# Threshold attention and hash-routed experts: GpSimd's indirect transfers given in other steps of a head pair

## The chip, the cores and the metric

The kernel runs on one core of one Trainium2 chip. The metric is device time in microseconds of one execution, and of several executions the median is given. A core has engines that run side by side, each with its own instruction queue, and wait for each other through semaphores: TensorE (PE: matrix products and transposes, into the accumulator memory PSUM), VectorE (DVE), ScalarE (ACT), GpSimd (POOL) and SyncE (SP), which here only issues transfers. SBUF is the on-chip working memory; DRAM tensors lie outside. In this kernel GpSimd computes small things and issues the indirect transfers, whose row addresses come from a table.

## The reference

Two blocks follow each other. The first is attention with a threshold, for 8 batches, 8 heads, 576 positions and a head width of 64. Of each row of scores only those within `tau` of the row's maximum count:

```python
scores = scale * np.matmul(q, k.transpose(0, 1, 3, 2))
thresh = np.max(scores, axis=-1, keepdims=True) - tau
scores = np.where(scores >= thresh, scores, -1000000000.0)
scores = scores - np.max(scores, axis=-1, keepdims=True)
attn = np.exp(scores)
attn = attn / (np.sum(attn, axis=-1, keepdims=True) + 1e-09)
return np.matmul(attn, v).astype(np.float32)
```

The result is laid out as `x`, 4608 tokens by 512. In the second block each token goes to one of 8 experts, chosen by its id alone:

```python
expert_idx = token_ids * np.int64(2654435761) % np.int64(E)
...
    h = np.maximum(xe @ w1[e], 0.0)
    out[mask] = h @ w2[e]
```

Since the choice of expert depends only on the ids, the routing can be worked out while attention still runs.

## The kernel before, in words

**Pairs and steps.** Attention works on two heads at a time. There are 32 head pairs: `p` counts them, eight batches for each of four pairs of heads (`hp`). A pair is worked in `NS = 5` steps, and one loop (L710) runs over all steps: `n` is the step in all, `p, s = divmod(n, NS)`, `LAST` is 160. Step 0 takes the last 64 query rows of both heads, steps 1 to 4 take 128 query rows each, for each head in turn. The order of instructions on every engine is the order in which this loop gives them (`manual_schedule`), so that the position of a line in the loop body is the position in the queue.

**The work on a step's rows.** `score` (L221) multiplies q and k on TensorE, one step ahead. `negate` (L238) on VectorE takes the scores from PSUM, negated, into `ns`, with their minimum in `nmx`; when a step's last head is negated, GpSimd adds the threshold, `thr` (L253). `expo` (L256) is the exponential on ScalarE. `mask` (L263) on VectorE multiplies the exponentials by the comparison with `thr` and sums them up. It is called one step later: in step n it works on step n-1, after the negations of step n. Two steps later `turn_w` (L285) transposes the weights on TensorE and `put_wT` (L294) copies them from PSUM on ScalarE. `av_part` (L305) multiplies them with v, `put_oT` (L327) copies out, `turn_o` (L331) transposes the result back in step 0 two pairs later, and `put_xm` (L347), in that same step 0, scales it on VectorE and writes it to the DRAM tensor `x_scratch` with three transfers on SP (L358, L363).

**SP's queue.** In step 0 of a pair, SP is given the loads of k and q for the pair after next (`load_pair`), those of v for the next pair (`load_v`), and after them x's writes. In step 2 of pairs 20 and 24 it is given the 2 MB load of the first and second expert's `w1`, in step 2 of pairs 22 and 26 those of `w2`.

**GpSimd's queue in a pair.** In step 1 it has `add_eps` (L338, two small operations) and `scale_k` (L214, k of the next pair), both ahead of that step's threshold. Each of the five steps has one threshold. At the end of a step, behind the threshold, stand the indirect transfers:

- *Scatters* (`scatters`, L539). When the route is known (`placed`), 36 scatters write token numbers into two slot tables in DRAM, alternately, one for each call. Each waits for the scatter before last, which wrote the same table. Behind them the same generator gives, at later calls, SP's reading of the tables and two small VectorE operations; then `routed` is set. `if s != 1 and placed` (L800) calls it in steps 0, 2, 3 and 4. The first scatter is that of pair 13, step 2, the last that of pair 22, step 0.
- *Early gathers* (`fetch_early`, L677). For the first expert, the first three quarters of its rows of x (`hp` 0 to 2; 5 groups of 128 slots, so 15 gathers of 64 KB) are fetched while the last quarter is still computed. A gather names all of `x_scratch`, so it waits for every write to it given before, and a write given after it waits for the gather. They start when `n > G0` (130, the start of pair 26), and are given in steps 3 and 4 (L802) and at the very start of step 0 (L713), ahead of that step's loads and of x's writes.

The last quarter's five gathers (L821) come when attention is over. Then follow the experts, 0 to 7, with loads, gathers and scatters of their own.

Of the kernel before, what the change touches and what calls it, by code (L numbers as in the profile page):

```python
# [20 lines left out]
def kernel(  # L21
# [29 lines left out]
    NS = 5  # L51
# [72 lines left out]
    def fetch_0(kt, hp):  # L124
        gather(x_rows, xg_bufs[kt][:, P * hp:P * hp + P], gidx_0[:, kt, hp:hp + 1])
# [18 lines left out]
    with tc.tile_pool(name="a_q", bufs=1) as a_q, \  # L144
# [59 lines left out]
        def load_v(p):  # L204
            hp, b = divmod(p, B)
            v_sb = v_bufs[p % 3]
            rows = v[b].rearrange("s h d -> s (h d)")[:, hp * P:hp * P + P]
            nc.sync.dma_start(out=v_sb[:, 0:4],
                              in_=rows[0:TAIL].rearrange("(c p) m -> p c m", p=P))
            for j in range(2):  # L210
                half = slice(64 * j, 64 * j + 64)
                nc.sync.dma_start(out=v_sb[half, 4, half], in_=rows[TAIL:S, half])
# [5 lines left out]
        def heads(n):  # L218
            return 1 if n % NS == 0 else 2
# [317 lines left out]
        placed, routed = [], []  # L537
# [139 lines left out]
        def fetch_early(n):  # L677


            if n > G0 and early:  # L680
                assert routed
                fetch_0(*early.pop(0))

        def fill(n):
            for _ in range(n):
                next(h_pieces, None)

        with tc.manual_schedule():
            make_identity(nc, ident[:])

            tr = ps_tr.tile([P, 2, 512], FP32, name="tr")
            for _ in range(17):
                nc.tensor.transpose(tr[:, 0, 0:P], ident[:], ident[:])
            nc.gpsimd.dma_start(out=tau_in[:],
                                in_=bass.AP(tensor=tau.tensor, offset=0, ap=[[0, P], [1, 1]]))

            nc.vector.tensor_scalar(out=k_scale[:], in0=tau_in[:], scalar1=0.0, scalar2=SCALE,
                                    op0=ALU.is_ge, op1=ALU.mult)  # L700
            nc.vector.tensor_scalar(out=kts[0][:, 0], in0=kts[0][:, 0], scalar1=k_scale[:],
                                    scalar2=None, op0=ALU.mult)
            nc.scalar.activation(kts[0][:, 1], kts[0][:, 1], AF.Copy, scale=k_scale[:])
            nc.vector.tensor_scalar(out=drop[:], in0=tau_in[:], scalar1=0.0, scalar2=3e38,  # L704
                                    op0=ALU.is_lt, op1=ALU.mult)
            nc.vector.tensor_tensor(out=drop[:], in0=drop[:], in1=tau_in[:], op=ALU.max)
            constants()
            next(pieces)
            score(0, 0)
            for n in range(LAST + NS + 1):  # L710
                p, s = divmod(n, NS)
                m = n - 2
                if s == 0:  # L713
                    fetch_early(n)
                if s == 0 and p + 2 < NP:
                    load_pair(p + 2)
                if s == 0 and p + 1 < NP:
                    load_v(p + 1)
                if s == 2 and p in (20, 24):
                    load_w1(p // 4 - 5)  # L720
                if s == 2 and p in (22, 26):
                    load_w2((p - 22) // 4)

                if (s == 3 and p > 0 or s == 2 and p in (9, 11, 13)) and not placed:
                    next(pieces)
                if s == 1 and 3 <= p < 2 + KT:
                    nc.sync.dma_start(out=xg_bufs[p - 2][:], in_=xg_bufs[0][:])

                if s == 1 and 2 + KT <= p < 2 + KT + N // DIN:
                    r0 = DIN * (p - 2 - KT)  # L730
                    nc.sync.dma_start(
                        out=x_dram[r0:r0 + DIN, DIN - P:].rearrange("(t p) m -> p t m", p=P),
                        in_=xg_bufs[0][:].rearrange("p (t m) -> p t m", m=P))
                q = p - 1
                if s == 1 and 0 <= q < NP:
                    add_eps(q)
                if s == (1 if p else 3) and p + 1 < NP:
                    scale_k(p + 1)
                if s == 2 and 0 <= q < NP:
                    nc.vector.reciprocal(recs[q][:], recs[q][:])  # L740
                if n == LAST + NS:
                    fill(2)
                if s == 0 and p >= 2:
                    turn_o()
                if n == LAST:
                    for k in (0, 2):
                        tr = ps_sc.tile([P, 2, 512], FP32, name="sc")
                        early_xT(tr, k, k + 2, 0, CO - 1)
                if s in (1, 2) and 0 <= q < NP and n != LAST + 1:
                    av_part(q, 0, ((0, 1, 2), (3, 4))[s - 1])  # L750
                if n < LAST and s in (1, 2):
                    negate(n, 0)
                    expo(n, 0)
                if s == 2 and 0 <= q < NP:
                    put_oT(0)
                if n > LAST:
                    fill(1)
                turned = 0 <= m < LAST
                if turned:
                    tr = turn_w(m, 0)  # L760
                    put_wT(m, 0, tr)
                if n == LAST:
                    put_xm(p - 2)
                    av_part(q, 0, (0, 1, 2))
                if n >= LAST:
                    fill(1)
                if n == LAST:
                    tr = ps_sc.tile([P, 2, 512], FP32, name="sc")
                    early_xT(tr, 4, 5, 0, CO - 1)
                if s in (3, 4) and 0 <= q < NP:  # L770
                    av_part(q, 1, ((0, 1, 2), (3, 4))[s - 3])
                if n < LAST and s not in (1, 2):
                    negate(n, 0)
                    expo(n, 0)
                if s == 0 and p > 0 and not placed:
                    next(pieces)
                if s == 0 and p >= 2 and n != LAST:
                    put_xm(p - 2)
                if s == 4 and 0 <= q < NP:
                    put_oT(1)  # L780
                if s in (3, 4) and turned:
                    tr = turn_w(m, 1)
                if n + 1 < LAST:
                    score(n + 1, 0)
                if s == 4 and turned:
                    put_wT(m, 1, tr)
                if n < LAST and heads(n) == 2:
                    negate(n, 1)
                    expo(n, 1)
                if s == 3 and turned:  # L790
                    put_wT(m, 1, tr)
                if n + 1 < LAST:
                    score(n + 1, 1)
                if s in (0, 1) and turned:
                    tr = turn_w(m, 1)
                    put_wT(m, 1, tr)
                if 0 < n <= LAST:
                    for j in range(heads(n - 1)):
                        mask(n - 1, j)
                if s != 1 and placed:  # L800
                    next(scatter_pieces, None)
                if s > 2:  # L802
                    fetch_early(n)
                if n == LAST:
                    fill(1)
            assert not early
            nc.vector.tensor_tensor(out=stok[:], in0=stok[:], in1=stok_odd[:], op=ALU.min)
            for h in range(4):
                rows, n = slice(32 * h, 32 * h + 32), (NB - h + 3) // 4
                nc.vector.tensor_copy(gidx[rows, 0:n], stok[rows, E - 1, h::4])  # L810
                nc.vector.tensor_copy(gidx[rows, KT - 1:KT],
                                      stok[rows, E - 1, NB - 4 + h:NB - 3 + h])
            for g in range(4):
                rows, n = slice(32 * g, 32 * g + 32), min(KT, NB - KT * g)
                nc.vector.tensor_copy(gidx_x[rows, 1:, 0:n], stok[rows, 1:, KT * g:KT * g + n])
            for _ in pieces:
                pass
            nc.vector.scalar_tensor_tensor(
                out=qidx[:], in0=stok[:], scalar=4.0,
                in1=quart[:, :, None].to_broadcast([P, E, NB]), op0=ALU.mult, op1=ALU.add)  # L820
            for kt in range(KT):  # L821
                fetch_0(kt, HP - 1)
            fill(FO * 2 * (CO - 1) - 18)
            tr = ps_tr.tile([P, 2, 512], FP32, name="tr")
            early_xT(tr, 0, KT, CO - 1, CO)
# [371 lines left out]
```

## Time and profile before

| | |
|---|---|
| median of 3 runs | 939.87 us (939.29 to 940.05) |
| the profiled execution | 931.3 us, its span 929.7 us |
| TensorE busy, matmul / weight load | 909.8 us (98%) / 662.0 us (71%) |
| VectorE busy | 757.5 us (81%) |
| ScalarE busy | 457.3 us (49%) |
| GpSimd busy | 403.7 us (43%) |
| scatters into the slot tables | 36, 45.0 us of GpSimd |
| early gathers and the last quarter's | 20, 24.6 us of GpSimd |

The page adds up one execution. Busy time is a mean over stages that differ: attention runs to about 460 us, the experts after that, and ScalarE, for one, has most of its work in the first half. A group's row gives the line of the kernel, the engine, the operation, what it writes and reads, how often, its busy time with the mean of one in ns, and the idle time of the engine just before it with what ended it. "issue" there means that nothing which the profile shows was waited for. For an indirect transfer the row's time is that of GpSimd, not that of the data. In a timeline, lines give start and duration in us, and idle time before in brackets.

### The profile page before, as it was taken

The numbers are of one execution on the slowest core, as the hardware profiler recorded it, in microseconds if no ns is written. First come the engines' busy times: TensorE is split into PE (matmuls) and PEld (weight loads), VectorE is DVE, ScalarE is ACT, GpSimd is POOL, SyncE is SP. The second block draws the span as 40 slices with busy tenths as digits, with TensorE's granted clock in tenths as the row PEclk, the third lists the DMA queues.
The fourth block names the chain that finished last, engine by engine and source line by source line (L and its number), as shares of the span: only waits on it lengthen the run. The fifth ranks groups of instructions, "written<-read, shape, count | busy, mean of one in ns | idle before, by whom it ended". The sixth has DMA issues, their size and how long they took to land.

```text
span 929.7 us, 20725 instructions
## 1 busy us (share of the span) xinstructions
PE 909.8 (98%) x7495; PEld 662.0 (71%) x7495; DVE 757.5 (81%) x1654; ACT 457.3 (49%) x741; POOL 403.7 (43%) x528
## 2 busy tenths in 40 slices
PE   7999999999999999999999999999999999999996
PEld 4666666656666566665678888788887978878785
DVE  7999999999999999999955776767668676777551
ACT  6888888888888898888812010110201021020110
POOL 4232432456666623455423370724527073440702
PEclk9999999999999999999999999999999999999999
DMA  7354463554545668743101745364372536412101
GB/s 175 92 148 118 109 152 93 136 131 103 123 105 153 159 165 214 216 107 88 30 25 51 237 131 158 133 173 141 95 223 75 164 133 165 157 34 50 48 3 55
DMA packets 114775, 113.11 MB, mean 122 GB/s; under 512 B 32475, under 2 KB 89315, under 8 KB 114672
## 3 DMA queue, kind: packets, MB, share of 16 engines
q1 hardware_dynamic: 105168, 92.64, 37.0%
q0 software_dynamic: 9072, 18.91, 7.0%
q8 instruction: 61, 1.00, 0.4%
q14 instruction: 42, 0.34, 0.1%
q10 hardware_dynamic: 432, 0.21, 0.1%
HBM read 81.99 MB, written 21.44 MB: 111 GB/s over the span
## 4 chain that ended last, share of the span: by engine, by line
PE 65%; issue 21%; POOL 7%; DVE 3%; ACT 2%; DMA 1%; another core or an unknown queue 1%; POOLq 0%; SPq 0%; DVEq 0%; ACTq 0%
PE av L313 18%; PE sc L235 15%; PE tr L282 11%; PE sc L941 9%; PE bank L941 8%; POOL out_dram L1036 6%; PE sc L640 2%; PE av L282 1%; POOL xg L119 1%; ACT w L260 1%; DVE ns L246 1%; DVE w L271 1%; ACT wT_b L303 1%; ACT wT_a L303 0%
## 5 line engine op out<-in xcount | busy, mean ns | idle before, releaser
L260 ACT ACTIVATE w<-ns,nmx 128x576 f32<-128x576 f32 x288 | 220.5, 777 | 28.8 <-DVE ns L246 27.8
L271 DVE SCALAR_TENSOR_TENSOR w<-ns,thr,w 128x576 f32<-128x576 f32 x288 | 225.8, 816 | 0.0
L1036 POOL DMA_INDIRECT out_dram<-o_q,qidx x127 | 138.1, 1087 | 191.7 <-DVE o_q L1028 153.1
L246 DVE TENSOR_SCALAR_CACHE_REDUCE ns<-sc 128x576 f32<-128x576 f32 x288 | 205.6, 747 | 8.1 <-PE sc L235 7.4
L253 POOL TENSOR_SCALAR thr<-nmx,drop 128x2 f32<-128x2 f32 (+1 forms) x160 | 104.4, 653 | 187.3 <-DVE ns L246 177.6
L235 PE MATMUL sc<-k_sb,q 64*128 64x288 f32 (+1 forms) x1280 | 179.2, 423 | 1.0 <-DVE drop L704 0.7
L282 PEld LDWEIGHTS tr<-ident,w 64*128 64x128 f32 x2624 | 106.0, 138 | 95.4 <-ACT wT_b L303 32.4
L282 PE MATMUL tr<-ident,w 64*128 64x64 f32 x2624 | 139.5, 231 | 6.0 <-ACT wT_b L303 2.6
L948 ACT ACTIVATE h<-h 128x576 f32<-128x576 f32 (+1 forms) x56 | 38.7, 693 | 164.8 <-DVE h L861 126.1
L235 PEld LDWEIGHTS sc<-k_sb,q 64*128 64x128 f32 (+1 forms) x1280 | 93.0, 177 | 23.2 <-DVE ns L246 9.4
L313 PE MATMUL av<-wT_a,v 128*64 128x320 f32 (+1 forms) x704 | 100.6, 418 | 0.2
L303 ACT COPY wT_a<-tr 128x512 f32<-128x512 f32 (+1 forms) x128 | 81.7, 638 | 20.7 <-PE tr L282 20.2
L303 ACT COPY wT_b<-tr 128x512 f32<-128x512 f32 (+1 forms) x128 | 81.4, 636 | 17.1 <-PE tr L282 11.2
L313 PE MATMUL av<-wT_b,v 128*64 128x256 f32 x640 | 83.2, 389 | 0.0
L313 PEld LDWEIGHTS av<-wT_a,v 128*64 128x64 f32 x704 | 43.8, 137 | 29.3 <-DVE xm L352 0.7
L951 ACT COPY p<-bank 128x576 f32<-128x576 f32 (+2 forms) x11 | 7.0, 633 | 99.5 <-PE bank L941 72.5
L313 PEld LDWEIGHTS av<-wT_b,v 128*64 128x64 f32 x640 | 40.2, 136 | 18.8 <-issue 0.7
L542 POOL DMA_INDIRECT slot_scratch<-tok,slot_i x36 | 45.0, 1251 | 9.4 <-issue 7.6
L941 PE MATMUL bank<-h,w_sb 128*128 128x288 f32 (+3 forms) x192 | 48.1, 404 | 0.0
L941 PE MATMUL sc<-h,w_sb 128*128 128x288 f32 (+3 forms) x192 | 47.7, 401 | 0.0
L941 PEld LDWEIGHTS bank<-h,w_sb 128*128 128x128 f32 x192 | 46.6, 300 | 0.5
L941 PEld LDWEIGHTS sc<-h,w_sb 128*128 128x128 f32 x192 | 45.9, 289 | 0.6
(197 smaller groups left out, 1303.7 us busy)
## 6 DMA issues: line engine op xcount, KB each, us to landing
w_sb<-in_moe_w_dram SPq DMA_DIRECT2D x16, 2048.0 KB
q<-in_q_dram SPq DMA_DIRECT2D x62, 288.0 KB
v<-in_v_dram SPq DMA_DIRECT2D x32, 256.0 KB
x_scratch<-xm SPq DMA_DIRECT2D x32, 256.0 KB
xT<-xq SPq DMA_DIRECT2D x84, 80.0 KB
k_sb<-in_k_dram SPq DMA_DIRECT2D x31, 144.0 KB
k_sb<-in_k_dram SPq DMA_DIRECT2D x32, 112.0 KB
x_scratch<-xg SPq DMA_DIRECT2D x9, 256.0 KB
```

What stands on the lines that cost most here:

```text
L235: nc.tensor.matmul(sc[out_rows, i, 0:S2], lhsT=q_sb[rows, h, q0:q1], rhs=k_sb[rows, h], start=True, stop=True)
L246: nc.vector.tensor_scalar(out=ns[:].rearrange("p (i s) -> p i s", i=2), in0=sc[:, :, 0:S2], scalar1=-1.0, scalar2=None, op0=ALU.mult, op1= ...
L253: nc.gpsimd.tensor_scalar(out=thr[:, 0:j + 1], in0=stats[n][0][:, 0:j + 1], scalar1=drop[:], scalar2=None, op0=ALU.add)
L260: nc.scalar.activation(w, nss[n, j][:], AF.Exp, bias=stats[n][0][:, j:j + 1], scale=-1.0)
L271: nc.vector.scalar_tensor_tensor(out=w, in0=nss.pop((n, j))[:], scalar=stats[n][1][:, j:j + 1], in1=w, op0=ALU.is_le, op1=ALU.mult, accum_ ...
L282: nc.tensor.transpose(dst[:, r, 64 * c:64 * c + 64], src[rows, c0:c0 + P], ident[rows, rows])
L303: nc.scalar.copy(dst, tr[:, :, 0:64 * n_c].rearrange("p r (c q) -> p r c q", c=n_c))
L313: nc.tensor.matmul(av[64 * j:64 * j + 64, g, c0:c1], lhsT=v_sb[:, c, 64 * j:64 * j + 64], rhs=wT[g][:, i, c0:c1], start=(c == 0), stop=stop)
L542: nc.gpsimd.indirect_dma_start(out=slot_dram[c % 2][:, :], out_offset=bass.IndirectOffsetOnAxis(ap=slot_i[:, c:c + 1], axis=0), in_=tok[:, ...
L941: nc.tensor.matmul(ps[:, i, 0:width], lhsT=lhsT, rhs=y[:, c], start=c == 0, stop=c == n_k - 1)
L948: nc.scalar.activation(c, c, AF.Relu)
L1036: inst = nc.gpsimd.indirect_dma_start(out=rows[:, :], out_offset=bass.IndirectOffsetOnAxis(ap=idx, axis=0), in_=o_sb, in_offset=None, boun ...
```

## The change

The generator of the scatters is called in steps 0 to 3 rather than in 0, 2, 3 and 4. Early gathers are given in steps 1, 2 and 3 rather than in 3, 4 and at the start of the next step 0; all of them now stand at the end of a step. Their number and order stay. The first scatter stays at pair 13, step 2; the last is now that of pair 22, step 1, and the calls that give SP's reading of the tables and that set `routed` fall in the same steps as before (pair 23, step 2, and pair 24, step 3). The gathers run in pairs 26 to 30, where before they ran from pair 26, step 3, to the start of pair 31.

```diff
@@ -710,8 +710,6 @@
             for n in range(LAST + NS + 1):
                 p, s = divmod(n, NS)
                 m = n - 2
-                if s == 0:
-                    fetch_early(n)
                 if s == 0 and p + 2 < NP:
                     load_pair(p + 2)
                 if s == 0 and p + 1 < NP:
@@ -797,9 +795,9 @@
                 if 0 < n <= LAST:
                     for j in range(heads(n - 1)):
                         mask(n - 1, j)
-                if s != 1 and placed:
+                if s < NS - 1 and placed:
                     next(scatter_pieces, None)
-                if s > 2:
+                if 0 < s < NS - 1:
                     fetch_early(n)
                 if n == LAST:
                     fill(1)
```

## The prediction

> **What bounds the kernel now.** The change touches attention only, so I read the page for that half, then GpSimd's groups, then timelines of single head pairs. Over the first 460 us, VectorE is the fullest engine: microsecond by microsecond from 374 to 420 us it is busy 44.94 of 46 us, TensorE's records 45.83 (but a busy PE is not PE at its peak), ScalarE 39.69, GpSimd 25.68. GpSimd has room; what matters is when it is busy.
>
> GpSimd's groups (busy us, mean ns | idle before, releasers):
>
> ```profile
> L253 POOL TENSOR_SCALAR thr<-nmx,drop 128x2 f32<-128x2 f32 (+1 forms) x160 | 104.4, 653 | 187.3 <-DVE ns L246 177.6 <-DVE pos L442 1.6 <-DVE oend L467 1.5
> L542 POOL DMA_INDIRECT slot_scratch<-tok,slot_i x36 | 45.0, 1251 | 9.4 <-issue 7.6 <-DMA slot_scratch<-tok,slot_i 1.8
> L119 POOL DMA_INDIRECT xg<-x_scratch,gidx x20 | 24.6, 1232 | 11.8 <-DMA x_scratch<-xm 7.1 <-issue 4.7
> ```
>
> A transfer holds GpSimd 1.0 to 1.4 us, and the thresholds (L253), which the masks need, queue behind it. Scatters lose 1.8 us to earlier scatters, gathers 7.1 us to x's writes.
>
> Let T0 be the start of a pair's first negation (L246, step 0). From VectorE's timeline, plain pairs (T0 332.64, 346.53, 360.42) have steps of 2.89, 2.22, 2.78, 3.10, 2.89 = 13.89 us. Pairs with scatters differ in the first: pair 18 (T0 261.08) has 3.23, 2.22, 2.79, 3.10, 2.89. The place, in the timeline of all engines, first of pair 18, then of plain pair 24:
>
> ```profile
> 260.68 1.30 POOL L542 DMA_INDIRECT slot_scratch<-tok,slot_i  x1 [0.16 <-issue]
> ...
> 261.31 0.41 PE L282 MATMUL tr<-ident,w 64*128 64x64 f32 x8
> ...
> 262.10 0.82 DVE L352 TENSOR_TENSOR xm<-av,rec 128x640 f32<-128x640 f32 x1 [0.25 <-issue]
> 262.19 0.58 ACT L303 COPY wT_b<-tr 128x512 f32<-128x512 f32 x1 [0.35 <-PE tr L282]
> ```
>
> ```profile
> 346.76 0.41 PE L282 MATMUL tr<-ident,w 64*128 64x64 f32 x8
> ...
> 347.21 0.82 DVE L352 TENSOR_TENSOR xm<-av,rec 128x640 f32<-128x640 f32 x1
> 347.27 0.59 ACT L303 COPY wT_b<-tr 128x512 f32<-128x512 f32 x1
> ```
>
> TensorE's turns start alike (T0+0.23), yet with a scatter given at the end of step 4, VectorE's xm and ScalarE's copy, both waiting for TensorE, start 0.12 and 0.21 us after that scatter's end (261.98). The copy lags at every step-4 transfer: it starts 0.10 to 0.23 us after its end in ten pairs, 0.4 to 0.6 us in three, and in pair 30 only after the next transfer too. After step 2 it does not: scatter 268.97 to 270.31, copy on time at 270.02. The rule I read off, with those four as exceptions: a TensorE result that comes due from about 1.0 us after a transfer's start to its end reaches its readers only after the end. Why, the trace doesn't say.
>
> **What the Trainium skill says.** "Perfetto Trace Analysis", DMA Instruction — SWDGE (GPSIMD): the recorded end is when descriptors are written, not when data has moved. The trace agrees: the gather of 403.91 ends at 404.93, but the x write on SP that waits for gathers is issued at 409.01. "SBUF — State Buffer", Who interferes with whom: ScalarE and TensorE never wait for GpSimd's port; a two-input VectorE operation contends only with a GpSimd operation that reads SBUF. The masks keep 0.81 us beside scatters, which agrees; ScalarE's lag shows that the port isn't the cause. "DMA: Bandwidth & Descriptors", Queues, rings and completion order: descriptors of one engine's queue are consumed in ring order. So x's write, given after the loads of q, k and v on SP, moves behind them. Same page, Anatomy of one DMA: completion waits for the write receipt. Here:
>
> ```profile
> 396.49 0.37 SPq L358 DMA_DIRECT2D x_scratch<-xm  x1
> 396.91 1.15 SPq L363 DMA_DIRECT2D x_scratch<-xm  x2
> ```
>
> ```profile
> 400.06 1.10 POOL L119 DMA_INDIRECT xg<-x_scratch,gidx  x1 [1.20 <-DMA x_scratch<-xm]
> ```
>
> 3.57 us from first issue to the waiting gather on an otherwise quiet queue (and 477.21 to 480.77), some 1.3 of it after the data has moved (by 398.7, from DMA shares by the microsecond).
>
> **The scatters.** 36 before and after, 4 a pair; the one of step 4 goes to step 1. No wait is new: each waits for the scatter two earlier, at least 5.2 us before now, 5.3 then.
> - Removed: the step-4 lag. Step 0 of pairs 14 to 22 exceeds 2.89 by 0.61, 0, 0.22, 0.72, 0.34, 0.36, 0.33, 0.10, 0.34: 3.02 us.
> - Removed: pair 21's waits for scatters slowed by the 2 MB weight load of pair 20 (landing 6.4 us after start). It costs 0.29 + 0.23 + 0.11 in steps 1 to 3: 0.63 us. In the new order the partners start 8 us apart across that load.
> - Added: the step-1 scatter. The threshold of step 1 ends at T0+5.23 (337.14+0.73), so the scatter runs T0+5.4 to 6.7, and the next threshold, free at T0+6.67, slips by 0.07. Its mask comes at T0+9.3: covered. Of TensorE's results, only av's end (T0+6.74, read by oT's copy at T0+6.88) is near the tail. I take 0.05 us x 9 pairs = 0.5; ends 0 and 0.33 x 9 = 3.0.
> Sum: 3.02 + 0.63 - 0.5 = 3.15 us gained.
>
> **The early gathers.** 15 of them: now at steps 3 and 4 and the start of the next step 0, then at steps 1, 2, 3 of pairs 26 to 30.
> - Removed: steps 0 to 2 of pairs 27 to 31 exceed a plain pair's by 0.42, 0.15, 0.15, 1.79, 0.01: 2.52 us. Most is pair 30, where two gathers in a row keep ScalarE's copy 1.87 us. That was seen once, so its gain could be 1.2 lower. The 0.1 in step 3 stays.
> - Added: a wait. The step-1 gather reads x_scratch, whose last write the same pair gives at step 0. SP issues it at T0+3.5 (336.12, pair 23), behind the loads; DMA is busy until T0+6.3, plus 1.3 gives a landing at about T0+7.6. GpSimd stands from T0+5.4, and behind it the threshold of step 2: gather 1.10, threshold 0.73, so T0+9.5 against a mask wanted at 355.85 - 346.53 = T0+9.32. VectorE stops 0.2 us in pair 26. Pair 27's loads share DMA with w2's 2 MB, busy to 394.4; with x's 1.2 us behind, landing 396.9 = T0+8.7: 1.3 us. Pairs 28 and 29: landing at T0+7.8 and 7.7, 0.4 and 0.3. Pair 30 loads no q or k, x goes at once: 0. Sum 2.2 us; below are 0 (early landing), above see the first rival. Later thresholds catch up: step 3's ends at about T0+11.7, wanted at 12.36.
> - SP: x's write waits for the last gathers (28.7 us in six waits now). Given two steps earlier they have landed, except perhaps pair 26's under w2; loads queued behind the write are a pair away.
> Sum: 2.52 - 2.2 = 0.3 us gained.
>
> The experts' stage behind attention has the same work, so it only shifts. Total 3.45 us. On the profiled execution, 931.3 us for a span of 929.7, that gives 927.9; the runs' median lies 8.6 us higher (939.87), and I apply the difference to it: 936.4.
>
> **Rivals.**
> Slower: the step-1 gathers' wait for x's write becomes the bound. Each us of landing past T0+7.4 stops VectorE one us in four pairs. Removed are 3.15 + 2.52 = 5.7 us, so it decides at a mean landing of T0+8.8; at T0+9.6 the four pairs lose 8.8, giving 943.0. For it: pair 27's T0+8.7, DMA shares near 1.0 for six us after T0. Against it: plain pair 23 has drained by T0+6.3.
> No change: the lag follows the transfer into step 1, 0.33 us in nine pairs, and pair 30's 1.8 us isn't typical: 3.65 - 3.0 + 1.3 - 2.2 = -0.2, so 940.1. For it: no transfer was ever at step 1, and four lags were longer than the tail. Against it: step 2 and 3 positions cost nothing.
> Faster still: x lands in time and pair 30's stall goes: 3.65 + 2.52 = 6.2, so 933.7.
>
> **How the numbers follow.** Forecast 0.50 (own range 934.8 to 938.0), faster still 0.12, no change 0.20, slower 0.18. 0.2% (1.9 us) is about what a measurement can tell here. Faster: 0.62 less a little of the forecast's upper edge, 0.60; slower 0.18; the rest, 0.22, within. The range goes from 933.5, at the faster-still case, to 941.5, inside the slower case, which leaves about one in ten on each side.
>
> **What would show it.** Right: xm no longer idles ahead of its start in pairs 14 to 22, step 0 back at 2.89, scatter-to-scatter waits gone; GpSimd's wait for x's writes grows from 7.1 us in 2 to about 16 in 5, and VectorE has gaps ahead of step 2's masks (L271) in pairs 26 to 29, longest in 27. Wrong: gaps of over 1 us there in every pair; or ScalarE's copies in steps 1 and 2 late after the new transfers; or pair 30 still long. SP's wait for gathers should shrink to below 10 us. What would break the forecast most is the landing time, which I have only from one plain pair and two quiet writes.

## The result, and the profile after

Over 20 executions of each, the changed kernel took 932.67 us in the median (929.88 to 938.12), the kernel before 935.06 us (931.09 to 940.05), a ratio of 0.9969 [0.9954, 0.9984]. That is 2.9 us faster by the ratio and 2.4 us by the medians, where 3.5 us were forecast. The forecast time of 936.4 us and its range from 933.5 us lie above the measured time all the same, because the median of three runs, 939.87 us, to which the difference was applied, was 4.8 us above the median of twenty. These three are among the twenty, and among the four longest of them; without them the median of before is 934.38 us, and the medians differ by 1.7 us.

That is not the whole result. On four other chips, where the kernel before takes 918.3 to 918.6 us, nothing of the gain is there: on the one of them where the whole change ran, it is slower, 1.0030 [1.0021, 1.0040]. On one more, where the kernel before takes 929.21 us (which chip the first comparison ran on is not on record; it may be the same), it is faster, 0.9970 [0.9947, 0.9993]. The granted clock doesn't make that difference: over its 20 executions there the change had 0.997 in the mean, as the kernel before had over 55. Ratios below are always within one chip.

The profiled execution after took 931.37 us, its span 929.8 us (before: 931.3 and 929.7). So the two profiled executions do not differ, and the reading has to go by stages. Here is where each pair begins (T0, its first negation), from VectorE's timelines, in us:

| | before | after | plain pairs of 13.89 |
|---|---|---|---|
| pairs 14 to 22 (scatters), nine pairs | 129.05 | 127.37 | 125.01 |
| pairs 26 to 30 (gathers), five pairs | 72.33 | 72.58 | 69.45 |
| T0 of pair 31 | 446.64 | 444.11 | |
| T0 of pair 31 to the end of the span | 483.1 | 485.7 | |

Up to pair 31 the change is 2.53 us ahead, 1.18 of them through pair 1 alone, which no edit touches (14.92 us before, 13.74 after; from 18 to 21 us TensorE's granted clock was 0.50 before and 1.00 after). The experts' stage, with the same work, is 2.6 us longer in the profile after and takes it back. Where the edits act, in the first two rows, 1.68 us are gained and 0.25 us lost.

GpSimd's groups after, in the columns of those of before (busy us, mean ns | idle before, releasers):

```profile
L253 POOL TENSOR_SCALAR thr<-nmx,drop 128x2 f32<-128x2 f32 (+1 forms) x160 | 98.9, 618 | 175.9 <-DVE ns L246 164.3 <-issue 2.1 <-DVE pos L442 1.6
L542 POOL DMA_INDIRECT slot_scratch<-tok,slot_i x36 | 46.0, 1277 | 9.8 <-issue 7.9 <-DMA slot_scratch<-tok,slot_i 1.9
...
L119 POOL DMA_INDIRECT xg<-x_scratch,gidx x20 | 26.1, 1306 | 21.4 <-DVE ns L246 10.1 <-DMA x_scratch<-xm 5.9 <-issue 3.0
```

The gathers' idle time went from 11.8 to 21.4 us. The 10.1 us put down to a negation are the waits ahead of the step-1 gathers of pairs 26 to 28 (3.49, 4.88 and 1.60 us) and one of 0.17 us; pair 29's, 2.25 us, is put down to a mask. The negations that GpSimd needed were long done by then, as the threshold ahead of the gather shows, so what ended these four waits, 12.2 us, is x's write. The 5.9 us under its own name are no early gather's: it is the wait of the last quarter's first gather, which the kernel before has too (5.9 of its 7.1 us). Together these are 18.2 us in five waits. What it cost VectorE stands in the page's row of the masks:

```profile
L271 DVE SCALAR_TENSOR_TENSOR w<-ns,thr,w 128x576 f32<-128x576 f32 x288 | 226.4, 818 | 3.2 <-POOL thr L253 3.2
```

The 3.2 us are in two places, 0.91 us in pair 26 and this one in pair 27 (T0 386.10), put together from the timelines of GpSimd, SP and VectorE:

```profile
390.59 0.73 POOL L253 TENSOR_SCALAR thr<-nmx,drop 128x2 f32<-128x2 f32 x1
...
390.99 0.37 SPq L358 DMA_DIRECT2D x_scratch<-xm  x1
...
396.20 1.10 POOL L119 DMA_INDIRECT xg<-x_scratch,gidx  x1 [4.88 <-DVE ns L246]
397.34 0.32 POOL L253 TENSOR_SCALAR thr<-nmx,drop 128x2 f32<-128x2 f32 x1
...
397.69 0.82 DVE L271 SCALAR_TENSOR_TENSOR w<-ns,thr,w 128x576 f32<-128x576 f32 x1 [2.27 <-POOL thr L253]
```

GpSimd is done with step 1's threshold at 391.32 and stands until x's write, issued at 390.99, has landed 5.2 us later. The threshold of step 2 is behind the gather, and VectorE waits 2.27 us for it. That write brings x of the last quarter (`hp` 3), which the early gathers don't read: they wait for it because a gather names the whole tensor.

The scatters: pair 18 after (T0 259.15), timeline of all engines, first the place that was late before, then that of step 2's scatter:

```profile
259.38 0.42 PE L282 MATMUL tr<-ident,w 64*128 64x64 f32 x8
...
259.84 0.82 DVE L352 TENSOR_TENSOR xm<-av,rec 128x640 f32<-128x640 f32 x1
259.89 0.59 ACT L303 COPY wT_b<-tr 128x512 f32<-128x512 f32 x1
```

```profile
266.83 1.32 POOL L542 DMA_INDIRECT slot_scratch<-tok,slot_i  x1 [0.16 <-issue]
...
267.22 0.44 PE L282 MATMUL tr<-ident,w 64*128 64x64 f32 x8
...
268.26 0.58 ACT L303 COPY wT_a<-tr 128x512 f32<-128x512 f32 x1 [0.45 <-PE tr L282]
```

VectorE's xm and ScalarE's copy are on time in step 0, as forecast, and step 0 is back at 2.89 us in every pair. But the same lateness now stands behind step 2's scatter: the turns end at 267.66, 0.83 us after the scatter's start, and the copy starts at 268.26, 0.11 us after the scatter's end (268.15). So it is in pairs 15 to 19 and 21, whose step 4 takes 3.13 to 3.32 us instead of 2.89; in pairs 14, 20 and 22, which have the same scatter there (that of pair 20 0.2 us later), it isn't.

The waits of a scatter for an earlier one are not gone: 1.8 us before, in pair 21, are 1.9 us after, 0.39 us at step 2 and 1.48 us at step 3 of pair 20. But pair 20 takes 13.89 us, so there they cost nothing.

SP's wait of x's write for the gathers shrank, here from the list of SP's waits (28.7 us in six before):

```profile
SPq L358 <- DMA xg<-x_scratch,gidx: 11.9, 4, 9.5
```

### The profile page after: what moved, and what is told of

The parts are those of the page before. It is cut to its first block, busy times and chain, and to the rows that moved or that the text cites. A ratio compares the mean times of both kernels' runs of the same rounds, so it can differ in the third digit from the quotient of the medians.

```text
span 929.8 us, 20725 instructions
## 1 busy us (share of the span) xinstructions
PE 908.1 (98%) x7495; PEld 662.0 (71%) x7495; DVE 756.8 (81%) x1654; ACT 456.7 (49%) x741; POOL 400.6 (43%) x528
## 4 chain that ended last, share of the span: by engine, by line
PE 59%; issue 22%; POOL 7%; DVE 5%; ACT 3%; DMA 1%; another core or an unknown queue 1%; SPq 0%; POOLq 0%; DVEq 0%; ACTq 0%
PE av L313 15%; PE sc L235 13%; PE tr L282 10%; PE sc L939 8%; PE bank L939 8%; POOL out_dram L1034 6%; PE sc L640 2%; DVE w L271 2%; ACT w L260 2%; PE av L282 1%; DVE ns L246 1%; ACT wT_a L303 1%; POOL xg L119 1%; DMA k_sb<-in_k_dram 1%
## 5 line engine op out<-in xcount | busy, mean ns | idle before, releaser
L253 POOL TENSOR_SCALAR thr<-nmx,drop 128x2 f32<-128x2 f32 (+1 forms) x160 | 98.9, 618 | 175.9 <-DVE ns L246 164.3
```

The source lines that it names most:

```text
L253: nc.gpsimd.tensor_scalar(out=thr[:, 0:j + 1], in0=stats[n][0][:, 0:j + 1], scalar1=drop[:], scalar2=None, op0=ALU.add)
```

## The experiments

The theory: scatters in step 4 make copies late, moving them gains; gathers in step 1 wait for x's write, which is behind v's loads on SP's queue. The rivals: the lateness belongs to any step that has a transfer, or to the chip; the gathers gain, or lose, by something else. Each diff below is against the kernel that is named.

### First chip of the experiments (kernel before: 918.42 us)

**Scatters alone moved**, against the kernel before:

```diff
-                if s != 1 and placed:
+                if s < NS - 1 and placed:
```

> The kernel before with the scatters alone moved (steps 0 to 3 rather than 0, 2, 3, 4); gathers stay. In the profile pairs 14 to 22 take 129.05 us before and 127.37 us after, plain pairs would take 125.01. Theory, the lag moves with the transfers: these pairs take about 127.4 us, step 0 at 2.89, and the copy after step 2's scatter late by 0.35 to 0.5 us in most pairs; pairs 26 to 30 stay at about 72.3 us; ratio to before about 0.998. Rival, all of the measured gain of 0.31% comes from the gathers: ratio 1.000. Rival, the lag was that of step 4 alone: 125.5 us, ratio 0.996.

Measured: 918.54 us, ratio 1.0004 [0.9995, 1.0012]. Pairs 14 to 22 take 13.88 to 13.90 us each. No gain, because there is no lateness to take away on this chip, as the next run shows.

**Gathers alone moved**, against the kernel before:

```diff
-                if s == 0:
-                    fetch_early(n)
...
-                if s > 2:
+                if 0 < s < NS - 1:
                     fetch_early(n)
```

> The kernel before with the early gathers alone moved (steps 1, 2, 3); scatters stay. Pairs 26 to 30 take 72.33 us before and 72.58 us after, plain ones would take 69.45. Theory, what the old places cost (pair 30 above all) and the new waits for x's writes cancel: pairs 26 to 30 at about 72.5 us with masks waiting 2 to 4 us for the threshold in pairs 26 and 27, ratio 1.000. Rival, the gathers bring the gain in most runs: ratio 0.997. Rival, the wait is worse in other runs: ratio 1.002.

Measured: 921.22 us, ratio 1.0029 [1.0018, 1.0040]. The scatters stand in the old steps here, step 4's among them, and pairs 14 to 22 still take 125.02 us together. Pair 26 takes 14.32 us, pair 27 15.65 us, the other three 13.88 to 13.90. These two pairs lose 2.0 us of the 2.8 through the step-1 gather, and nothing is gained against it. In the profile the experts' stage is longer too (478.8 us against 477.6 with the scatters alone moved); what makes it so is not shown.

**Other places**, against the changed kernel: scatters in steps 0, 1 and (two) 3, gathers in step 2 and (two) 3, so that no gather comes early enough to wait for x:

```diff
-                if s < NS - 1 and placed:
+                for _ in range((1, 1, 0, 2, 0)[s] if placed else 0):
                     next(scatter_pieces, None)
-                if 0 < s < NS - 1:
+                for _ in range((0, 0, 1, 2, 0)[s]):
                     fetch_early(n)
```

> The changed kernel with one scatter in steps 0 and 1 and two in step 3, none in step 2; early gathers one in step 2 and two in step 3, none in step 1. Theory, only the transfer's place against TensorE's turns counts, and a gather given one step later finds x's write landed before a mask needs the threshold: pairs 14 to 22 at about 125.5 us, pairs 26 to 30 at about 70, ratio to before 0.993 to 0.995. Rival, four transfers a pair cost some 0.35 us wherever they stand, and two in a row hold the copies of step 4: pairs 14 to 22 at 127.5 or more, pairs 26 to 30 at 72, ratio 0.997 or above.

Measured: 918.52 us, ratio 1.0006 [0.9998, 1.0014]. Pairs 26 to 30 take 13.88 to 14.05 us. One step later, the same 15 gathers cost nothing in the profile.

**x's write ahead of v's loads** on SP, against the changed kernel, from pair 2 on:

```diff
-                if s == 0 and p + 1 < NP:
+                if s == 0 and p < 2:
                     load_v(p + 1)
...
+                    if p + 1 < NP:
+                        load_v(p + 1)
```

> The changed kernel, but in step 0 SP is given v's loads after x's write and not before it. Theory, the step-1 gather waits because x's write stands behind the loads in SP's queue: 288 KB less ahead of it lets it land about 1.2 us earlier; the gathers of pairs 26 and 27 start at about T0+7.5 and T0+8.9 (8.72 and 10.10 in the changed kernel), the masks' wait for the threshold falls from 3.2 us to about 1, pairs 26 to 30 take about 70.7 us instead of 72.6, ratio to before 0.995. Rival, it waits for w2's 2 MB load on the same DMA engines or for the completion: starts and pairs unchanged within 0.3 us, ratio 0.997.

Measured: 919.25 us, ratio 1.0008 [1.0002, 1.0015]. Pair 27 in the timelines of SP, GpSimd and VectorE, first with the gathers alone moved (T0 383.54), then with x's write first (T0 383.15):

```profile
385.14 1.95 SPq L212 DMA_DIRECT2D v<-in_v_dram  x2
387.92 0.37 SPq L358 DMA_DIRECT2D x_scratch<-xm  x1
...
393.38 1.10 POOL L119 DMA_INDIRECT xg<-x_scratch,gidx  x1 [4.61 <-DVE ns L246]
...
394.87 0.82 DVE L271 SCALAR_TENSOR_TENSOR w<-ns,thr,w 128x576 f32<-128x576 f32 x1 [2.00 <-POOL thr L253]
```

```profile
386.88 0.38 SPq L358 DMA_DIRECT2D x_scratch<-xm  x1
...
388.55 1.00 SPq L208 DMA_DIRECT2D v<-in_v_dram  x1
...
391.79 1.10 POOL L119 DMA_INDIRECT xg<-x_scratch,gidx  x1 [3.41 <-DVE w L271]
...
393.28 0.82 DVE L271 SCALAR_TENSOR_TENSOR w<-ns,thr,w 128x576 f32<-128x576 f32 x1 [0.74 <-POOL thr L253]
```

The gather starts at T0+8.64 instead of T0+9.84. Of these 1.20 us, 0.65 is the earlier issue (T0+3.73 against 4.38), 0.55 the shorter way to the landing, with v's 288 KB behind it and no longer ahead. Pairs 26 and 27 take 13.90 and 14.45 us. That the gather's start follows x's write is thereby shown; it also agrees with the Trainium skill, "DMA: Bandwidth & Descriptors", Queues, rings and completion order, after which descriptors of one engine's queue are consumed in order.

### Second chip (before: 918.52 us)

**The change again, and the kernel before again**, neither altered.

> The whole change once more, unaltered, on the chip of this call. Theory: its gain in the first comparison was the late copies and masks at the scatters, which that chip's executions had and the chip of the first four experiments did not. Where the profile of the kernel before shows pairs 14 to 22 at 13.9 us each (no late copies), the change only adds the masks' wait of about 2.2 us in pairs 26 and 27, and the ratio is 1.0025 to 1.003. Where it shows them at 14.2 to 14.5 us, the ratio is again 0.996 to 0.998. Rival (the parts gain together, by something that neither part shows alone): a ratio of 0.996 to 0.998 with pairs 14 to 22 at 13.9 us in both kernels.

> The kernel before, unaltered, for its profile on the chip of this call, where its steps can be set beside those of the other kernels. Theory: with no late copies at the scatters, pairs 14 to 22 last 13.88 to 13.90 us each, 125.0 us together (129.05 in the first profile), pair 30 is at 13.9 us (15.78 in the first profile), and the head-pair stage from pair 1 to pair 31 is some 6 us shorter than in the first profile. Rival (the lateness belongs to the kernel and was taken away by the edits of each experiment): pairs 14 to 22 sum to 128 to 130 us here too.

Measured: the change 921.25 us, 1.0030 [1.0021, 1.0040]; the kernel before against itself 918.39 us, 0.9998 [0.9989, 1.0007]. Pairs 14 to 22 take 125.00 us with the change and 125.01 without, pairs 26 to 30 72.42 and 69.74: 2.68 us lost there, against 2.73 between the medians. The place of step 2's scatter in pair 18 of the change, on this chip (T0 258.30):

```profile
265.97 1.32 POOL L542 DMA_INDIRECT slot_scratch<-tok,slot_i  x1 [0.16 <-issue]
...
266.36 0.44 PE L282 MATMUL tr<-ident,w 64*128 64x64 f32 x8
...
266.90 0.58 ACT L303 COPY wT_a<-tr 128x512 f32<-128x512 f32 x1
```

Scatter, turns and copy are given at the same offsets as in the first profile after; here the copy starts 0.10 us after the turns' end, 0.39 us before the scatter's. The late masks are here as on the other chips:

```profile
394.37 1.10 POOL L119 DMA_INDIRECT xg<-x_scratch,gidx  x1 [4.51 <-DVE ns L246]
395.51 0.32 POOL L253 TENSOR_SCALAR thr<-nmx,drop 128x2 f32<-128x2 f32 x1
...
395.86 0.82 DVE L271 SCALAR_TENSOR_TENSOR w<-ns,thr,w 128x576 f32<-128x576 f32 x1 [1.90 <-POOL thr L253]
```

**Other places again**, and **a busy GpSimd in place of step 4's scatter**, against the kernel before:

```diff
+                if c % 4 == 2:
+                    nc.gpsimd.memset(h_0[:, 0:2], 0.0)
+                    yield
+                    continue
```

> The scatters in steps 0, 1 and 3 (two of them there), the early gathers in steps 1, 2 and 3 as one, one and two less those that waited: the placing of the third experiment again. Theory: same as before within 0.1 per cent where the kernel before has no late copies; 0.994 to 0.996 where it has them, since it is then ahead of the change by the 2.2 to 3.2 us of the masks' wait. Rival: slower than before by the gathers' wait wherever they are early, ratio 1.002 or more.

> In the kernel before, the nine scatters of step 4 are left out, and GpSimd fills a small tile in their place for about 1.2 us, with no transfer; the tokens of those nine scatters are missing in the output. Theory A (the copies are late because GpSimd is executing anything at that time): where the kernel before shows late copies after the scatters, they stay, pairs 14 to 22 at 128 us or more together. Theory B (they are late because of the indirect transfer, its descriptors or its landing): they go, 125.0 us. On a chip where the kernel before has no late copies the two agree: 125.0 us, and the run says only that the scatters' nine transfers cost nothing there, a ratio of 0.999 to 1.001.

The text on the other places, here and on the later chips, names step 1 for the gathers as well; the edit is that of the first chip, which gives none there.

Measured: other places 918.57 us, 1.0001 [0.9993, 1.0010]. The fill for the scatter: pairs 14 to 22 125.02 us, which tells nothing here, since the kernel before has no lateness on this chip. Its time, 926.53 us, is 8 us longer, all of it after T0 of pair 31 (439.33 against 439.31 before), where the experts work from slot tables with nine scatters missing; I haven't looked into that.

### Third chip (before: 929.21 us)

**The change, and the scatters alone**, once more; and the scatters alone with **a fill ahead of step 2's**, which starts that scatter 0.2 us later:

```diff
                 if s < NS - 1 and placed:
+                    if s == 2:
+                        nc.gpsimd.memset(h_0[:, 0, 0:200], 0.0)
                     next(scatter_pieces, None)
```

The fill goes on in step 2 up to pair 31 and there overwrites part of the first expert's hidden values (`h_0`); only pairs 14 to 22 are read from it.

> The whole change on whatever chip this call gets. Theory: two kinds of chip, told by the level of the kernel before. At 918 to 919 us (as in the two calls so far) no copy is late at a transfer, pairs 14 to 22 take 125.0 us and the ratio is 1.0025 to 1.003. At 931 us or more (as in the first comparison) the copies are late and the ratio is 0.996 to 0.998. Rival: level and ratio are not tied, and the ratio is 0.996 to 0.998 at a level of 918 us.

> The scatters alone moved to the first four steps of a pair. Theory: at a level of 918 us for the kernel before, a ratio of 0.9995 to 1.0005, no gain and no loss. At a level of 931 us or more, the late copies go from step 4 to step 2 in some pairs, pairs 14 to 22 take 127 to 127.5 us where the kernel before takes 129, and the ratio is 0.998. Rival: the step that holds a scatter is worth something by itself, and the ratio is under 0.999 at a level of 918 us too.

> The scatters alone moved, with a fill on GpSimd ahead of step 2's scatter, which starts it some 0.25 us later. Theory: on a chip with late copies, step 2's copy of w is late by what the later end of the scatter adds, 0.7 to 0.8 us instead of 0.52 us, and every pair shows it; on one without, pairs 14 to 22 stay at 13.89 us each. Rival (TensorE or ScalarE makes the copy late by itself): the lateness stays where it was, 0.5 us, with the scatter's end after the copy's start.

Measured: the change 927.35 us, 0.9970 [0.9947, 0.9993]; the scatters alone 928.44 us, 0.9983 [0.9965, 1.0000]; with the fill 928.15 us, 0.9991 [0.9970, 1.0012]. With the level, the lateness is back. (The kernel before has no profile on this chip, so what each edit saved there is known from the times alone, and the intervals of the last two reach 1.) In the change, pair 18 (T0 258.91):

```profile
266.60 1.32 POOL L542 DMA_INDIRECT slot_scratch<-tok,slot_i  x1 [0.16 <-issue]
...
266.97 0.44 PE L282 MATMUL tr<-ident,w 64*128 64x64 f32 x8
...
268.00 0.59 ACT L303 COPY wT_a<-tr 128x512 f32<-128x512 f32 x1 [0.43 <-PE tr L282]
```

The copy starts 0.08 us after the scatter's end (267.92). This time pairs 16, 18, 20 and 21 are the late ones (nine pairs: 126.64 us), with the scatters alone pairs 18, 20 and 21 (125.99). With step 2's scatter 0.2 us later only pairs 15 and 21 are (126.14); there the copies start 0.21 and 0.25 us after the scatter's end, not at it. I had expected every pair to be late and by more: that was wrong. Neither the pair nor the amount is fixed by the place in the program.

What the old places of the gathers cost on such a chip, this shows: pair 30 with the scatters alone moved, the gathers as before, on this chip (T0 426.47), and then pair 30 of the kernel before on the second chip (T0 425.43), both from the timeline of all engines:

```profile
426.76 0.46 PE L282 MATMUL tr<-ident,w 64*128 64x64 f32 x8
...
427.69 0.82 DVE L352 TENSOR_TENSOR xm<-av,rec 128x640 f32<-128x640 f32 x1 [0.46 <-issue]
427.74 1.01 POOL L119 DMA_INDIRECT xg<-x_scratch,gidx  x1 [0.30 <-issue]
...
429.16 0.59 ACT L303 COPY wT_b<-tr 128x512 f32<-128x512 f32 x1 [1.78 <-PE sc L235]
```

```profile
425.65 0.42 PE L282 MATMUL tr<-ident,w 64*128 64x64 f32 x8
...
426.11 0.82 DVE L352 TENSOR_TENSOR xm<-av,rec 128x640 f32<-128x640 f32 x1
426.21 0.58 ACT L303 COPY wT_b<-tr 128x512 f32<-128x512 f32 x1
...
426.70 1.00 POOL L119 DMA_INDIRECT xg<-x_scratch,gidx  x1 [0.30 <-issue]
```

On the second chip the copy starts 0.14 us after the turns' end and 0.49 us before the second gather; on the third it starts 1.94 us after the turns' end, when both gathers are over (the second ends at 428.75), and pair 30 takes 15.72 us instead of 13.88, as in the first profile of before (15.78). The change takes that away (14.15), pays its masks' wait in pairs 26 and 27 (15.05 and 15.85), and its five pairs take 72.93 us, against 72.17 with the gathers left in their places.

**The experts' stage** shows the same lateness. Set beside the same kernel on the second chip, instruction by instruction, VectorE in the change on this chip is 2.4 us behind at 459 us and 9.7 us at 846 us, which is the whole difference of the two spans (929.2 and 919.5 us). Of the 7.3 us between, 6.6 come in two stretches, 545 to 576 us and 809 to 846 us, where VectorE and ScalarE wait for TensorE beside a row of GpSimd's transfers. (Of these 6.6 us, 1.8 are indirect: in the first stretch TensorE runs dry for 2.09 us, and its granted clock is then 0.50 from 564 to 566 us.) From the timelines of all engines, the first of these places, on this chip and then on the second:

```profile
550.77 1.62 PE L939 MATMUL sc<-xT,w_s 128*128 128x288 f32 x6
...
556.16 1.00 POOL L119 DMA_INDIRECT xg<-x_scratch,gidx_x  x1 [0.30 <-issue]
...
559.32 0.76 DVE L859 TENSOR_TENSOR h<-sc,u 128x576 f32<-128x576 f32 x1 [5.99 <-remote]
```

```profile
548.17 1.13 PE L939 MATMUL sc<-xT,w_s 128*128 128x288 f32 x4
...
549.34 0.76 DVE L859 TENSOR_TENSOR h<-sc,u 128x576 f32<-128x576 f32 x1
```

VectorE reads a product that TensorE has finished at 552.39, and starts 6.93 us later, 2.16 us after the last of five gathers in a row; on the second chip it starts 0.04 us after the product's end. "remote" means that the view finds no instruction which ended the wait. The trace also records when TensorE's semaphore rises: at 559.29 here and at 549.32 there, and for pair 18's turns above at 267.92 (their end 267.41) and at 266.82 (266.80). TensorE has gone on to its next products by then (the one after starts at 552.23), so what comes late is the signal that its result is there; neither TensorE nor the reader is slow. All five profiles of the higher level have this place, with 4.5 to 6.0 us of idle time and a start 2.11 to 2.17 us after the last gather's end.

### Fourth and fifth chip (before: 918.32 and 918.61 us)

The cause of the lateness was still open, so the kernel before, the busy GpSimd, the gathers alone and the other places ran on two more chips. The edits are those above.

> The kernel before, unaltered, for its profile on the chip of this call. Theory: at a level of 918 to 919 us, pairs 14 to 22 take 125.0 us and pair 30 takes 13.9 us; at 925 us or more, copies and negations after step 4's scatter are late in most of the nine pairs, 127.5 to 129.5 us together, and pair 30 takes 15.7 us as in the profile with the scatters alone moved. Rival: the level has nothing to do with it, and pairs 14 to 22 take 125.0 us at a high level.

> Step 4's nine scatters left out again (their tokens are missing in the output), a fill of 1.2 us on GpSimd in each one's place, with no transfer. Theory A (GpSimd's execution at that time makes the copies late): at a level of 925 us or more, step 0 of pairs 14 to 22 stays at 3.2 us or more in most pairs, 127.5 us or more together. Theory B (the indirect transfer does): step 0 is at 2.89 us in all, and the nine pairs take 125.0 to 126 us, what is left being the scatters of the other steps. At 918 us both give 125.0 us.

> The gathers alone moved. Theory: the masks of pairs 26 and 27 wait 2.2 to 3.2 us on any chip. At a level of 925 us or more, the 1.8 us of pair 30 and some 0.9 us of late copies in pairs 27 to 29 are saved, and the two cancel: ratio 0.999 to 1.001. At 918 us nothing is saved: ratio 1.0025 to 1.003. Rival (the gathers are what gains where the level is high): ratio under 0.998 there.

> Scatters in steps 0, 1 and 3 (two there), gathers in steps 1 and 2, with the last two of a pair in step 3: no mask waits for them. Theory: at a level of 925 us or more it keeps the change's saving and is spared its masks' wait of 2.2 to 3.2 us, so a ratio of 0.994 to 0.996; at 918 us, 1.0000 to 1.0006. Rival: two scatters in step 3 bring late copies there, and it gains no more than the change, 0.997.

> The kernel before, unaltered, for its profile on the chip of this call. Theory as for the last such run: at a level of 925 us or more, pairs 14 to 22 take 127.5 to 129.5 us together and pair 30 takes 15.7 us; at 918 to 919 us, 125.0 and 13.9 us. Rival: 125.0 us at a high level too.

> Step 4's nine scatters left out (their tokens are missing in the output), a fill of 1.2 us on GpSimd in their place. Theory A (GpSimd's execution makes the copies late): at a level of 925 us or more, pairs 14 to 22 take 127.5 us or more, step 0 is at 3.2 us in most. Theory B (the indirect transfer does): step 0 at 2.89 us in all, 125.0 to 126 us together. At 918 us both give 125.0 us.

> Scatters in steps 0, 1 and 3 (two there), gathers in steps 1 and 2, with the last two of a pair in step 3. Theory: at a level of 925 us or more, the change's saving without its masks' wait, a ratio of 0.994 to 0.996; at 918 us, 1.0000 to 1.0006. Rival: two scatters in step 3 bring late copies there, and it gains no more than the change, 0.997.

Both chips were of the lower level. Measured:

| | us | ratio | pairs 14 to 22 | pairs 26 to 30 |
|---|---|---|---|---|
| before, fourth chip | 918.79 | 1.0002 [0.9993, 1.0011] | 125.00 | 69.61 |
| busy GpSimd, fourth | 927.02 | 1.0093 [1.0075, 1.0111] | 124.99 | 69.62 |
| gathers alone, fourth | 921.24 | 1.0027 [1.0017, 1.0037] | 125.01 | 71.88 |
| other places, fourth | 918.51 | 1.0004 [0.9996, 1.0012] | 125.01 | 69.59 |
| before, fifth | 918.60 | 0.9998 [0.9989, 1.0007] | 125.01 | 69.76 |
| busy GpSimd, fifth | 927.03 | 1.0090 [1.0071, 1.0108] | 125.05 | 69.77 |
| other places, fifth | 918.89 | 1.0003 [0.9994, 1.0011] | 125.03 | 69.62 |

The masks' wait is confirmed a third time. The level and the lateness go together in every profile there is: five profiles at a level of 929 us or more (the first two and the third chip's three) have late copies, with 126.0 to 129.1 us for nine pairs; the other fifteen have none, with 125.0 to 125.2. Whether GpSimd's execution or the transfer makes a copy late where it happens, and whether the other places would gain there, was not tried on such a chip: on the one that there was, other kernels ran. Two readings speak against execution as such. In plain pairs of the higher level GpSimd executes its small operations almost without a break from 335.70 to 337.87 us (pair 23 of before), and these pairs take 13.89 us; and at the place shown in the experts' stage the lateness outlasts GpSimd's execution by 2.16 us. Both questions stay open.

## Why the prediction was right or wrong

**The level.** The failed step is "the runs' median lies 8.6 us higher (939.87), and I apply the difference to it". The median of twenty runs of before is 935.06 us. With it the same sum gives 931.6 us, 1.1 us from what was measured. That the difference itself, 3.45 us, lies near the 2.9 us of the ratio is partly luck: in the profiles its two terms came to 1.68 us where 3.15 were forecast, and to 0.25 us lost where 0.3 were to be gained. The range was built around a difference and didn't hold the uncertainty of the level: single executions on that chip are spread over 8 to 9 us, and three of them within 0.8 us of each other gave a false certainty. The profiled execution of 931.3 us, in the same material, had said so.

**The scatters.** "Removed: the step-4 lag" came true: step 0 is at 2.89 us in all nine pairs. Pair 21 no longer loses time to waits for scatters, but not because "the partners start 8 us apart": the waits went to pair 20, where nothing waits for them; and in the profile of before on the fourth chip pair 21 has such waits of 0.94 and 0.72 us and takes 13.90 us. The sum of 3.15 us was not: 1.68 us in the profiles. What failed is the rule I read off, that a result due from about 1.0 us after a transfer's start is late and that "step 2 and 3 positions cost nothing". The lateness went to step 2's copy in six of nine pairs (due 0.83 us after the start in pair 18), which the no-change rival foresaw in kind, but at step 1. And the deeper premise, that the lateness is a property of the program, fell: at 918 us both kernels have none, and the scatters alone moved gain -0.4 us [-1.1, +0.5] (ratio 1.0004).

**The gathers.** Forecast were 2.52 - 2.2 = 0.3 us gained; the profiles show 0.25 us lost. The mechanism was right: GpSimd waits for x's writes in five places (18.2 us, forecast about 16), the longest gap is in pair 27, pair 30 is freed. Mis-sized was the term "landing 396.9 = T0+8.7: 1.3 us": the gather started at T0+10.10, and VectorE lost 2.27 us. x's write was issued at T0+4.9 (390.99), not at T0+3.5 as in plain pair 23, and took 5.2 us to its landing, where 3.57 had been measured on a quiet queue. Pair 26 had 0.91 us instead of 0.2 (landing T0+8.7 instead of 7.6). Pairs 28 and 29, forecast at 0.4 and 0.3, lost nothing (T0+6.83 and 7.48). SP's wait for gathers was to fall below 10 us; it is 11.9.

**The rivals.** The slower one decides on the three chips of the lower level where the change or its gathers ran (1.0027 to 1.0030). Its point of decision, a mean landing at T0+8.8, was worked out against 5.7 us of removed lateness; on a chip without that, any landing past T0+7.4 decides, and two pairs are enough for 1.003. Its place was right, and its price nearly so: pair 27's gather at T0+9.84 with the gathers alone moved, 2.4 us past T0+7.4, cost a wait of 2.00 us. Its condition was one that the profile of one chip couldn't show.

**What is left over.** On the chips of the higher level the ratio says 2.9 us (1.5 to 4.3) and 2.8 us (0.7 to 4.9) gained, while the medians differ by 2.4 and 1.9 us and the profiles of the first comparison show 1.43 us in the two stages concerned. Lateness differs from profile to profile there, so one profile of each may just be off; that the rest is of this kind is an argument and not shown. The experts' stage takes 479.7 to 486.0 us at the higher level, against 477.3 to 478.8 at the lower (the runs with scatters missing aside), and in the third chip's profile of the change most of that is lateness at GpSimd's transfers too. Of what makes the lateness, and why one chip has it and another not, no run says anything.

## What to carry to other kernels

Before you sell a wait that the profile shows, ask whether it is made by the program or by the chip: look for the same instruction at the same offset on time elsewhere (step 0 exceeded a plain pair's by 0.61, 0 and 0.22 us in pairs 14 to 16), and take a second chip before you call it a bound. A transfer that is moved ahead on an in-order engine must be checked against the landing of what it names, under the heaviest load of that stretch, and it is worth asking whether it must name so much (a gather that doesn't name the last quarter wasn't tried): here one step later (step 2 instead of 1) the same gathers cost nothing. And a level belongs to as many runs as its spread asks for; forecast a ratio, and let the range hold the level's doubt.

## What was not expected of the hardware

Six comparisons fell into two levels, 918.3 to 918.6 us and 929.2 to 935.1 us for the same kernel, and TensorE's granted clock doesn't explain it: at a clock of 0.998, 16 executions on the third chip have a median of 929.02 us, 12 on the fourth one of 918.24 us. The level is, for the most part, the lateness itself: between the two profiles of the change on the second and third chip it makes up all but about 1 us of 9.7, if the 1.8 us of slower clock that follow it once are counted in. Executions of the kernel before are spread over 1.7 to 2.8 us at the lower level and over 9 to 14 us at the higher; part of the latter goes with the clock (the change in the first comparison: 937.34 us at 0.993, 929.88 us at 0.998).

At the higher level, instructions of ScalarE and VectorE that wait for TensorE start, in part of the pairs, only after an indirect transfer of GpSimd has ended. In attention that is mostly 0.05 to 0.25 us after, and up to 1.8 us late where two transfers follow each other; in the experts' stage it is up to 6 us late in a row of transfers. They need nothing of these transfers; TensorE's semaphore itself rises late. At the lower level the same instructions are on time under the same transfers.

Pair 1 takes 14.90 to 14.92 us in four of the twenty profiles and 13.73 to 13.75 us in the others, at both levels. The granted clock makes the difference: in those four it was 0.50 for three microseconds, from 18 to 21 us, and in the other sixteen it stayed at 1.00 there. One and the same kernel, that of the other places, has 13.75 us in one profile and 14.91 in another: 1.2 us that a comparison of two single profiles would have given to the change.
